# V products of a segment-recurrent attention in column tiles: two units side by side for the segment's tokens, four for the memory's, with a new order of stages

## The chip, the cores and the metric

The kernel runs on one core of one Trainium2 chip. The metric is the device time of one execution in microseconds (us). Engines: TensorE (PE, matmuls; PEld are its weight loads), VectorE (DVE), ScalarE (ACT), GpSimd (POOL) and SyncE (SP, which only issues DMA transfers here). PSUM is the memory that matmuls write, SBUF the on-chip memory that everything else works in.

## The reference

Two layers alternate, twice: A, B, A, B. A is attention over segments with a recurrent memory, B is a local dilated attention. Cut to what matters:

```python
def _A_ref(x, mem0, Wq, Wk, Wv, Wo, seg_len):       # S = 2048, Dm = 640, 32 heads of 192, M = 8, seg_len = 32
    mem = mem0
    for s in range(n_seg):                           # 64 segments, one after the other
        h = concat([mem, x[:, s*seg_len:(s+1)*seg_len]])   # 40 tokens
        q, k, v = h @ Wq, h @ Wk, h @ Wv             # each 40 x 6144
        p = softmax(where(mask, q k^T * scale, -1e9))
        o = (p v) @ Wo
        mem = o[:, :M]                               # the next segment needs it
        outs.append(o[:, M:])

def _B_ref(x, wqkv, wo):                             # 32 heads of 20, window of 8 tokens at distance 2
    ...

x = x + _A_ref(layernorm(x), ...)
x = x + _B_ref(layernorm(x), ...)
x = x + _A_ref(layernorm(x), ...)
x = x + _B_ref(layernorm(x), ...)
```

All weights are bfloat16. Wq, Wk, Wv and Wo of layer A are 31 MB together, more than fits on the chip beside the rest.

## The kernel before

The two A layers run as two **lanes** (index `l`) in one pass: lane 0 works on segment s of the first A layer, lane 1 on segment s - 2 (`LAG = 2`) of the second. So each weight that is loaded serves 2 x 40 = 80 token columns. There are 66 steps with attention (numbered 0 to 65) and one last step that only finishes layer B.

The weights of A are cut into 64 **halves** of 128 x 1920 bfloat16 (491,520 bytes): halves 0 to 31 hold Wk and Wq in turn (32 heads are 16 pairs, called units, of 384 columns), 32 to 47 Wv, 48 to 63 Wo. 31 halves stay in SBUF (`res`); 33 are streamed again in every step through a ring of five buffers (`wt`), as two DMA transfers each, which SP issues in the order of use. In step 0 all halves are read from the inputs, and the streamed ones are written back to `Wr` in the layout in which later steps read them. From then on the loads come from `Wr`.

A step is the list `ORDER`, which fixes the order of TensorE's instructions and of SP's transfers by hand; the instructions of VectorE, ScalarE and GpSimd are put in order by the framework's scheduler. Each engine works through its list strictly in order. The words of the list:

- `q0` to `q15`: K and Q of one unit, 30 matmuls of 80 columns each (L303 for q0, L308 for the others); ScalarE copies the result to one of five `QK` buffers (L310).
- `v0` to `v15`: V of one unit. The stationary operand is the state `ST`, 128 columns wide: two lanes in slots of 64, of which 40 are tokens. Five matmuls of 384 columns (L356); ScalarE copies the even units, VectorE the odd ones (L360, L362).
- `s0` to `s3`: scores of four units, in 64 x 64 and 128 x 64 tiles of the array (L320, L326), then the softmax on VectorE (L330 to L338) with the exp on ScalarE (L334).
- `t0` to `t3`: four transposes of the probabilities (L345); two copies to `PT` (L347 on VectorE, L348 on ScalarE).
- `pv0` to `pv3`: probabilities times V (L373), 128 x 64 tiles in pairs; ScalarE copies the result to `ot` (L376).
- `o0` to `o14`: the product with Wo, accumulated in `acc` (L390); o14 takes halves 62 and 63.
- Layer B: `ln1` (L278, L279), `qkv` (L438, copies L440, products L445 on VectorE and GpSimd), `logits` (L454 in 128 x 32 tiles, four side by side, softmax L465 to L473 with the exp L467 on ScalarE), `e0` to `e4` (the weights spread to all channels, L480, then product and sum on VectorE, L483 and L485), `wo` (L492), `ln2` (state of lane 1 for the next step), `store`.
- `alpha` writes the segment's tokens of lane 0 to the next `ST` on GpSimd; `input` prepares 128 tokens in every fourth step from `x_sb`, which SP loads.

At the end of a step VectorE casts the memory columns of `acc` into the next `ST` (L401); the next q0 waits for it. All PSUM tiles but `acc` come from one pool of six buffers (`ps`), used in turn. The code of the order:

```python
ORDER = """
q0 v0 q1 ln10 alpha0 q2 v1 input0 q3 v2 s0 q4 qkv0 v3 t0 q5 q6 v4 q7 v5 logits0
s1 pv0 q8 o0 o1 v6 q9 e0 t1 v7 q10 o2 o3 e1 q11 v8
s2 pv1 q12 e2 o4 o5 v9 q13 e3 t2 v10 o6 o7 q14 e4 v11 q15 v12
s3 pv2 wo0 o8 v13 v14 ln20 t3 v15 store0 o9 o10 pv3 o11 o12 o13 o14
"""
```

The functions that the change touches:

Of the kernel before, what the change touches and what calls it, by code (L numbers as in the profile page):

```python
# [10 lines left out]
BF16 = mybir.dt.bfloat16  # L11
F32 = mybir.dt.float32
# [21 lines left out]
NQK = 5  # L34
OUT_CHUNKS = ((0, 1, 2), (3, 4))
# [13 lines left out]
N_RESIDENT = 31  # L49
# [11 lines left out]
def stages():  # L61

    names = ("alpha", "ln1", "qkv", "logits", "input", "wo", "ln2", "store", "pv", "q", "s", "t", "v", "o", "e")
# [26 lines left out]
def window1(ap, c):  # L90

    v = ap[:, c, :, 0:SEG]
    dims = [list(x) for x in v.ap]
    return bass.AP(v.tensor, v.offset, dims[:2] + [[BDIL, BW]] + dims[2:])

# [11 lines left out]
class Kernel:  # L107
    def __init__(self, ctx, tc, A_x, A_mem0, A_Wq, A_Wk, A_Wv, A_Wo, B_wqkv, B_wo, out):
        self.tc, self.nc = tc, tc.nc
        self.x = A_x[0, :, :]  # L110
        self.out = out[0, :, :]
        self.S = A_x.shape[1]
        self.n_seg = self.S // SEG
        self.Wq, self.Wk, self.Wv = (w.rearrange("d h e -> d (h e)") for w in (A_Wq, A_Wk, A_Wv))
        self.Wo = A_Wo.rearrange("h e d -> (h e) d")
        self.B_wqkv, self.B_wo, self.mem0 = B_wqkv, B_wo, A_mem0[0, :, :]
        pool = lambda name, bufs, **k: ctx.enter_context(tc.tile_pool(name=name, bufs=bufs, **k))
        self.cp = pool("consts", 1)
# [6 lines left out]
        self.vp = pool("vp", 6)  # L125
        self.psC = pool("psC", 1, space=PSUM)
        self.ps = pool("ps", 6, space=PSUM)


    def constants(self):  # L130
# [47 lines left out]
        self.ST = [cp.tile([P, NCH, 2, SLOT], BF16, name=f"ST{i}") for i in range(2)]  # L178
# [5 lines left out]
        self.Pm = [cp.tile([P, 4, 2, SLOT], BF16, name=f"Pm{i}") for i in range(2)]  # L184
# [3 lines left out]
        for t in self.PT:  # L188
            nc.gpsimd.memset(t[:], 0.0)
        self.zero = cp.tile([P, NCH, SEG], BF16, name="zero")  # L190
# [8 lines left out]
        nc.vector.tensor_copy(out=self.ST[0][:, :, 0, 0:NM], in_=mt[:, :, :])  # L199
# [63 lines left out]
    def alpha_x(self, s):  # L263

        xt = self.xt[s // 4]
        o = SEG * (s % 4)
        self.nc.gpsimd.tensor_copy(out=self.ST[s % 2][:, :, 0, NM:LT], in_=xt[0][:, :, o:o + SEG])
# [27 lines left out]
    def qk(self, i):  # L295
        nc = self.nc
        st = self.ST[self.step % 2]
        ps = self.ps.tile([P, 6, 2, LT], F32, name="qk_ps", tag="ps")
        w = [self.half(2 * i + k)[:, :].rearrange("p (c n) -> p c n", c=NCH) for k in range(2)]
        if i == 0:  # L300
            for c in range(NCH):
                for m in range(6):
                    nc.tensor.matmul(ps[:, m, :, :], lhsT=w[m // 3][:, c, (m % 3) * P:(m % 3 + 1) * P], rhs=st[:, c, :, 0:LT],  # L303
                                     start=(c == 0 and m == 0), stop=(c == NCH - 1), skip_group_check=True)
        else:
            for m in range(6):
                for c in range(NCH):
                    nc.tensor.matmul(ps[:, m, :, :], lhsT=w[m // 3][:, c, (m % 3) * P:(m % 3 + 1) * P], rhs=st[:, c, :, 0:LT],  # L308
                                     start=(c == 0), stop=(c == NCH - 1))
        nc.scalar.copy(out=self.QK[i % NQK][:, 0:12 * LT], in_=ps[:, :, :, :].rearrange("p m l t -> p (m l t)"))  # L310

    def scores(self, g):
# [25 lines left out]
        nc.vector.tensor_tensor(out=self.Pm[g % 2][:, :, :, 0:LT].rearrange("p a l t -> p (a l) t"), in0=sb[:, :, :],  # L338
                                in1=sm[:, :].unsqueeze(2).to_broadcast([P, 8, LT]), op=ALU.mult)

    def p_transpose(self, g):
        nc = self.nc
        ps = self.ps.tile([P, 4, 2, SLOT], BF16, name="pt_ps", tag="ps")
        for j in range(4):
            nc.tensor.transpose(out=ps[:, j, :, :].rearrange("p h q -> p (h q)"),  # L345
                                in_=self.Pm[g % 2][:, j, :, :].rearrange("p l t -> p (l t)"), identity=self.ident[:, :])
# [3 lines left out]
    def v(self, i):  # L350
        nc = self.nc
        w = self.half(32 + i)[:, :].rearrange("p (c n) -> p c n", c=NCH)
        st = self.ST[self.step % 2]
        ps = self.ps.tile([P, UW], F32, name="v_ps", tag="ps")
        for c in range(NCH):
            nc.tensor.matmul(ps[:, :], lhsT=st[:, c, :, :].rearrange("p l t -> p (l t)"), rhs=w[:, c, :],  # L356
                             start=(c == 0), stop=(c == NCH - 1))
        vt = self.vp.tile([P, UW], BF16, name="vt")
        if i % 2 == 0:
            nc.scalar.copy(out=vt[:, :], in_=ps[:, :])  # L360
        else:
            nc.vector.tensor_copy(out=vt[:, :], in_=ps[:, :])  # L362
        self.vts[i] = vt

    def pv(self, g):
        nc = self.nc
        for k in (2 * g, 2 * g + 1):
            ps = self.ps.tile([P, 2, 3, 2, LT], F32, name="o_ps", tag="ps")
            for jj in range(2):
                i = 2 * k + jj  # L370
                vt = self.vts.pop(i)
                for (n, slot, h, col) in ((0, 0, 0, 0), (0, 1, 0, 64), (1, 0, 0, 128), (1, 1, 1, 192), (2, 0, 1, 256), (2, 1, 1, 320)):
                    nc.tensor.matmul(ps[64 * slot:64 * (slot + 1), jj, n, :, :], lhsT=vt[:, col:col + 64], rhs=self.PT[g % 2][:, i % 4, h, :, :],  # L373
# [19 lines left out]
    def finish_step(self):  # L393
        nc, s = self.nc, self.step
        nxt = self.ST[(s + 1) % 2]
# [28 lines left out]
    def b_qkv(self):  # L424
        nc = self.nc
        qT = self.w1.tile([P, NCH, 2, SEG], BF16, name="qT", tag="q")
        kh = self.w2.tile([P, NCH, 2, BPAD + SEG], BF16, name="kh")
        vh = self.w2.tile([P, NCH, 2, BPAD + SEG], BF16, name="vh")
        for new, old in ((kh, self.kh), (vh, self.vh)):
            if old is None:  # L430
                nc.gpsimd.memset(new[:, :, :, 0:BPAD], 0.0)
            else:
                nc.gpsimd.tensor_copy(out=new[:, :, :, 0:BPAD], in_=old[:, :, :, SEG:SEG + BPAD])
# [7 lines left out]
        self.qT, self.kh, self.vh = qT, kh, vh  # L441
# [63 lines left out]
    def beta_x(self):  # L505
# [4 lines left out]
        self.ln_apply(self.x2_next[:, :, :], m, r, self.ST[(self.step + 1) % 2][:, :, 1, NM:LT], SEG)  # L510
# [14 lines left out]
    def run(self):  # L525
        nc, tc = self.nc, self.tc
        self.resident, self.xt, self.vts, self.ots = {}, {}, {}, {}
        self.Wr = {h: self.dram.tile([P, HALF], BF16, name=f"Wr{h}") for h in range(N_HALVES) if h not in RESIDENT}
        self.kh = self.vh = None
        self.x2 = self.x2_next = None  # L530
        self.step = 0
        with tc.manual_schedule(engines={PE, SP}):
# [5 lines left out]
            attend = {"q": self.qk, "s": self.scores, "t": self.p_transpose, "v": self.v, "pv": self.pv, "o": self.o}  # L538
# [80 lines left out]
```

## Time and profile before

| | |
|---|---|
| median of 3 runs (lowest, highest) | 3518.95 us (3516.27, 3520.65) |
| the profiled execution: its time, its span | 3520.67 us, 3519.0 us |
| step 0 (until the first q0 of step 1 starts) | 145.4 us |
| matmuls of V, L356 | 3630 with streamed, 1650 with resident weights, 328 ns each |
| ScalarE's copies: QK (L310), ot (L376), V (L360) | 557, 559, 481 ns each |
| VectorE's copy of V (L362) | 550 ns each |
| HBM read | 1091.68 MB, 316 GB/s over the span |

The span runs from the first instruction to the last. A row of a timeline or of the chain gives the start in us, the busy time in us, the engine (PE) and source line, what is written and read, and "x" the count; in brackets stands how long the engine had been idle and what ended that. The duration of a matmul includes its way through the array: matmuls overlap, and the distance from one group's start to the next one's is what a group costs. "37 ns a pair" and the like are such distances divided by counts.

### The profile page before, as it was taken

Reading aid. Unit: us, or ns where it says so; the run is one execution under the profiler, and the core shown is the slowest. Engines: PE = TensorE matmul, PEld = TensorE weight load, DVE = VectorE, ACT = ScalarE, POOL = GpSimd, SP = SyncE. Lnnn points to the kernel's source line nnn. Section 1 sums busy time; section 2 is a strip of 40 time slices with the busy share of each in tenths; the row PEclk is TensorE's granted clock in tenths of the full one; section 3 lists DMA queues with packets and bytes.
Section 4 is the critical chain, followed back from the end, with each engine's and each line's share of the span. In section 5 each row is a group of like instructions: output and inputs, shape, how many; then the busy total and the mean of one; then the engine's idle time right before and its main releaser. Section 6 shows DMA issues by size and latency. Waiting matters only on the chain.

```text
span 3519.0 us, 172521 instructions
## 1 busy us (share of the span) xinstructions
PE 3388.8 (96%) x78044; PEld 2891.7 (82%) x78045; DVE 2197.2 (62%) x5056; ACT 1479.6 (42%) x3213; POOL 369.9 (11%) x467
## 2 busy tenths in 40 slices
PE   5799999999999999999999999999999999999997
PEld 3588888888888888888888888888888888888886
DVE  1366666666666666666666666666666666666665
ACT  1244444444444444444444444444444444444443
POOL 2110110010111011001101101110010111011000
PEclk7799999999999999999999999999999999999998
DMA  9999999999999999999999999999999999999995
GB/s 350 352 321 320 318 320 315 316 320 323 319 323 317 317 314 322 320 322 319 322 326 322 324 322 320 318 324 326 321 319 323 315 320 324 320 317 319 319 320 202
DMA packets 664961, 1121.84 MB, mean 319 GB/s; under 512 B 70744, under 2 KB 661472, under 8 KB 664224
## 3 DMA queue, kind: packets, MB, share of 16 engines
q1 hardware_dynamic: 659280, 1091.96, 92.5%
q0 software_dynamic: 2640, 16.22, 1.1%
q8 instruction: 610, 9.99, 1.1%
q10 hardware_dynamic: 2304, 2.62, 0.2%
q14 instruction: 127, 1.04, 0.1%
HBM read 1091.68 MB, written 18.84 MB: 316 GB/s over the span
## 4 chain that ended last, share of the span: by engine, by line
PE 83%; DMA 9%; DVE 4%; ACT 2%; SPq 1%; issue 1%; ACTq 0%; POOLq 0%; POOL 0%; DVEq 0%
PE qk_ps L308 29%; PE v_ps L356 21%; PE acc L390 13%; DMA wt<-Wr 4%; PE qkv_ps L438 4%; PE o_ps L373 3%; PE s_ps L326 3%; PE s_ps L320 3%; PE qk_ps L303 2%; PE bc_ps L480 2%; DMA x_sb<-in_A_x_dram 2%; PE pt_ps L345 1%; DMA wt<-in_A_Wv_dram 1%; SPq L214 1%; PE y_ps L492 1%
## 5 line engine op out<-in xcount | busy, mean ns | idle before, releaser
L310 ACT CAST QK<-qk_ps 128x480 bf16<-128x480 f32 x1056 | 581.5, 557 | 1042.7 <-PE qk_ps L308 828.5
L356 PE MATMUL v_ps<-wt,ST 128*128 128x384 bf16 x3630 | 717.4, 328 | 13.9 <-DMA wt<-in_A_Wv_dram 9.2
L308 PE MATMUL qk_ps<-ST,wt 128*128 128x80 bf16 x14850 | 687.8, 203 | 22.6 <-DMA wt<-in_A_Wq_dram 10.6
L308 PE MATMUL qk_ps<-ST,res 128*128 128x80 bf16 x14850 | 691.4, 202 | 18.1 <-DMA res<-in_A_Wq_dram 9.4
L308 PEld LDWEIGHTS <-wt 128*128 128x128 bf16 x14850 | 610.1, 100 | 78.8 <-DMA wt<-in_A_Wq_dram 11.8
L356 PEld LDWEIGHTS <-ST 128*128 128x128 bf16 x5280 | 466.1, 99 | 246.6 <-issue 16.4
L308 PEld LDWEIGHTS <-res 128*128 128x128 bf16 x14850 | 610.9, 100 | 48.9 <-DMA res<-in_A_Wq_dram 10.4
L390 PE MATMUL acc<-ot,res 128*128 128x80 bf16 x9900 | 465.6, 202 | 17.4 <-DMA res<-in_A_Wo_dram 9.6
L390 PEld LDWEIGHTS <-res 128*128 128x128 bf16 x9900 | 409.9, 100 | 38.3 <-DMA res<-in_A_Wo_dram 11.8
L362 DVE CAST vt<-v_ps 128x384 bf16<-128x384 f32 x528 | 290.2, 550 | 210.0 <-PE v_ps L356 209.8
L483 DVE TENSOR_TENSOR prod<-bc_ps,vh 128x512 bf16<-128x512 f32 x330 | 227.3, 689 | 245.0 <-PE bc_ps L480 244.4
L360 ACT CAST vt<-v_ps 128x384 bf16<-128x384 f32 x528 | 253.7, 481 | 244.8 <-PE v_ps L356 243.2
L485 DVE TENSOR_REDUCE oT<-prod 128x64 bf16<-128x512 bf16 x330 | 336.7, 1021 | 4.5
L356 PE MATMUL v_ps<-res,ST 128*128 128x384 bf16 x1650 | 326.8, 329 | 2.7 <-DMA res<-in_A_Wv_dram 2.7
L390 PE MATMUL acc<-ot,wt 128*128 128x80 bf16 x5940 | 309.9, 202 | 6.2 <-DMA wt<-in_A_Wo_dram 3.5
L376 ACT CAST ot<-o_ps 128x480 bf16<-128x480 f32 x528 | 268.4, 559 | 109.3 <-PE o_ps L373 109.3
L330 DVE TENSOR_TENSOR sb<-s_ps,maskA 128x320 f32<-128x320 f32 x264 | 129.7, 491 | 253.7 <-PE s_ps L326 253.6
L390 PEld LDWEIGHTS <-wt 128*128 128x128 bf16 x5940 | 261.3, 100 | 18.1 <-issue 4.7
L445 POOL TENSOR_TENSOR prod<-qT,kh 128x1280 bf16<-128x1280 bf16 x66 | 169.9, 2575 | 653.0 <-ACT kh L440 653.0
L348 ACT COPY PT<-pt_ps 64x320 bf16<-64x320 bf16 x264 | 110.9, 420 | 296.7 <-DVE PT L347 295.1
L273 POOL TENSOR_TENSOR sq<-x 128x160 f32<-128x160 bf16 x64 | 28.9, 452 | 1837.4 <-DVE x L496 1837.4
L445 DVE TENSOR_TENSOR prod<-qT,kh 128x1280 bf16<-128x1280 bf16 x66 | 201.2, 3048 | 3.4 <-ACT kh L440 3.4
(117 smaller groups left out, 3709.3 us busy)
## 6 DMA issues: line engine op xcount, KB each, us to landing
wt<-Wr SPq DMA_DIRECT2D x4290, 240.0 KB, 4.8
Wr<-wt POOLq DMA_DIRECT2D x33, 480.0 KB, 6.7
wt<-in_A_Wv_dram SPq DMA_DIRECT2D x11, 480.0 KB, 10.5
res<-in_A_Wo_dram SPq DMA_DIRECT2D x10, 480.0 KB, 10.8
wt<-in_A_Wk_dram SPq DMA_DIRECT2D x9, 480.0 KB, 11.1
res<-in_A_Wq_dram SPq DMA_DIRECT2D x9, 480.0 KB, 11.3
res<-in_A_Wk_dram SPq DMA_DIRECT2D x7, 480.0 KB, 10.2
wt<-in_A_Wq_dram SPq DMA_DIRECT2D x7, 480.0 KB, 10.2
```

The source lines that it names most:

```text
L308: nc.tensor.matmul(ps[:, m, :, :], lhsT=w[m // 3][:, c, (m % 3) * P:(m % 3 + 1) * P], rhs=st[:, c, :, 0:LT], start=(c == 0), stop=(c == NC ...
L310: nc.scalar.copy(out=self.QK[i % NQK][:, 0:12 * LT], in_=ps[:, :, :, :].rearrange("p m l t -> p (m l t)"))
L330: nc.vector.tensor_tensor(out=sb[:, :, :], in0=sv, in1=self.maskA[:, :].unsqueeze(1).to_broadcast([P, 8, LT]), op=ALU.add)
L356: nc.tensor.matmul(ps[:, :], lhsT=st[:, c, :, :].rearrange("p l t -> p (l t)"), rhs=w[:, c, :], start=(c == 0), stop=(c == NCH - 1))
L360: nc.scalar.copy(out=vt[:, :], in_=ps[:, :])
L362: nc.vector.tensor_copy(out=vt[:, :], in_=ps[:, :])
L376: nc.scalar.copy(out=ot[:, :, :, :], in_=ps[:, :, :, :, :].rearrange("p j n l t -> p (j n) l t"))
L390: nc.tensor.matmul(a[:, at, :, :], lhsT=w[h][:, m, dc * P:(dc + 1) * P], rhs=self.ots[h // 2][:, 3 * (h % 2) + m, :, :], start=(h == 0 and ...
L438: nc.tensor.matmul(ps[:, d, :, :], lhsT=self.wqkv[:, c, kind * D + d * P:kind * D + (d + 1) * P], rhs=self.xnB[:, c, :].rearrange("p (l t) ...
L445: eng.tensor_tensor(out=self.prod[:, :, l, :, :], in0=qT[:, :, l, :].unsqueeze(2).to_broadcast([P, NCH, BW, SEG]), in1=window(kh, l), op=A ...
L483: nc.vector.tensor_tensor(out=pv, in0=ps[:, :, :, :], in1=window1(self.vh, c), op=ALU.mult)
L485: nc.vector.tensor_reduce(out=self.oT[:, c, :].rearrange("p (l t) -> p l t", l=2), in_=pv.rearrange("p l w t -> p l t w"), op=ALU.add, axi ...
```

## The change

Three things change together, and two follow from them.

1. **Token layout.** `ST` becomes 96 columns wide: 16 columns of zeros, then 40 tokens with the two lanes interleaved (token 0 of lane 0, token 0 of lane 1, and so on): columns 16 to 31 are the memory of both lanes, 32 to 95 the segments of both. q reads 80 contiguous columns, and its ScalarE copy puts the lanes apart again while it reads PSUM.
2. **V in column tiles.** For each group g of four units there are three stages. `va` and `vb` take two units each: the 64 segment columns are the stationary operand of two tiles, 128 x 64 at array columns 0 and 64, and each tile is fed its own unit's weights. `vc` takes the 32 columns of zeros and memory with four units in 128 x 32 tiles. Results go to one buffer `V` with rows chosen per unit (`SEG_ROW`, `MEM_ROW`); all eight copies of a group are on ScalarE. The probabilities are written to the matching columns of `Pm` in two VectorE operations instead of one, and `PT` is made by two VectorE operations that mask by lane, in place of one copy each on VectorE and ScalarE.
3. **New order and 32 resident halves.** V stands in one block behind each s and pv, so the other stages move; 32 halves stay in SBUF, 32 are streamed, another set than before: of Wv only 33, 35, 38, 41 and 46. `kh` and `vh` of layer B become fixed buffers instead of two that alternate, and GpSimd copies their tails in place.

```diff
-N_RESIDENT = 31
+N_RESIDENT = 32
+PAD = 2 * NM
+MID = 2 * PAD
+WIDE = PAD + 2 * LT
+SEG_ROW = (0, 64, 0, 64)
+MEM_ROW = (64, 0, 96, 32)
...
 ORDER = """
-q0 v0 q1 ln10 alpha0 q2 v1 input0 q3 v2 s0 q4 qkv0 v3 t0 q5 q6 v4 q7 v5 logits0
-s1 pv0 q8 o0 o1 v6 q9 e0 t1 v7 q10 o2 o3 e1 q11 v8
-s2 pv1 q12 e2 o4 o5 v9 q13 e3 t2 v10 o6 o7 q14 e4 v11 q15 v12
-s3 pv2 wo0 o8 v13 v14 ln20 t3 v15 store0 o9 o10 pv3 o11 o12 o13 o14
+q0 q1 ln10 alpha0 q2 input0 q3 s0 va0 vb0 vc0 qkv0 q4 t0 q5 q6 q7
+s1 pv0 va1 vb1 vc1 logits0 q8 o0 q9 t1 o1 e0 q10 o2 e1 o3 q11
+s2 pv1 va2 vb2 vc2 e2 q12 o4 q13 e3 t2 q14 o5 e4 q15 wo0
+s3 pv2 va3 vb3 vc3 o6 o7 ln20 store0 t3 o8 o9 pv3 o10 o11 o12 o13 o14
 """
...
-STREAMED = (
-    0, 2, 5, 7, 8, 9, 11, 12, 14, 16, 18, 21, 22, 25, 27, 30, 34, 35, 37, 38, 39, 40, 42, 43, 44, 45, 47, 53, 54,
-    56, 58, 60, 63,
-)
+STREAMED = (1, 5, 6, 7, 8, 11, 13, 14, 15, 17, 22, 23, 25, 26, 29, 30, 31, 33, 35, 38, 41, 46, 48, 49, 50, 51, 53, 55, 56, 58, 60, 63)
...
+def tokens(t):
+
+    return t[:, :, PAD:].rearrange("p c (t l) -> p c l t", l=2)
...
-        nc.scalar.copy(out=self.QK[i % NQK][:, 0:12 * LT], in_=ps[:, :, :, :].rearrange("p m l t -> p (m l t)"))
+        nc.scalar.copy(out=self.QK[i % NQK][:, 0:12 * LT].rearrange("p (m l t) -> p m l t", m=6, l=2), in_=ps[:, :, :, :].rearrange("p m t l -> p m l t"))
...
-        nc.vector.tensor_tensor(out=self.Pm[g % 2][:, :, :, 0:LT].rearrange("p a l t -> p (a l) t"), in0=sb[:, :, :],
-                                in1=sm[:, :].unsqueeze(2).to_broadcast([P, 8, LT]), op=ALU.mult)
+        at = [P * j + SEG_ROW[j] for j in range(4)]
+        am = [P * j + MEM_ROW[j] + PAD for j in range(4)]
+        for o, t, n in ((at, NM, SEG), (am, 0, NM)):
...
+            nc.vector.tensor_tensor(out=out, in0=strip(sb[:, :, :], t, [[4 * LT, 2], [2 * LT, 2], [1, n], [LT, 2]]),
+                                    in1=strip(sm[:, :], 0, [[4, 2], [2, 2], [0, n], [1, 2]]), op=ALU.mult)
...
-        nc.vector.tensor_copy(out=self.PT[g % 2][0:64, :, :, 0, :], in_=ps[0:64, :, :, 0:LT])
-        nc.scalar.copy(out=self.PT[g % 2][64:128, :, :, 1, :], in_=ps[64:128, :, :, 0:LT])
+        for l in range(2):
+            nc.vector.tensor_scalar(out=self.PT[g % 2][:, :, :, l, :], in0=ps[:, :, :, 0:LT], scalar1=self.maskL[:, l:l + 1], scalar2=None, op0=ALU.mult)
...
-        for c in range(NCH):
-            nc.tensor.matmul(ps[:, :], lhsT=st[:, c, :, :].rearrange("p l t -> p (l t)"), rhs=w[:, c, :],
-                             start=(c == 0), stop=(c == NCH - 1))
...
+    def v_seg(self, g, a):
...
+        for c in range(NCH):
+            for j in units:
+                r = SEG_ROW[j]
+                nc.tensor.matmul(ps[r:r + 64, :], lhsT=st[:, c, MID:WIDE], rhs=self.wv[j][:, c, :],
+                                 start=(c == 0), stop=(c == NCH - 1), tile_position=(0, r), skip_group_check=True)
+        for j in units:
+            r = SEG_ROW[j]
+            nc.scalar.copy(out=self.V[r:r + 64, j, :], in_=ps[r:r + 64, :])
+
+    def v_mem(self, g):
...
+        for c in range(NCH):
+            for j in range(4):
+                r = MEM_ROW[j]
+                nc.tensor.matmul(ps[r:r + 32, :], lhsT=st[:, c, 0:MID], rhs=self.wv[j][:, c, :],
+                                 start=(c == 0), stop=(c == NCH - 1), tile_position=(0, r), skip_group_check=True)
+        for j in range(4):
+            r = MEM_ROW[j]
+            nc.scalar.copy(out=self.V[r:r + 32, j, :], in_=ps[r:r + 32, :])
```

The words of the new list stand for `va`, `vb` (`v_seg` with a = 0 and 1) and `vc` (`v_mem`) of one group; the others mean what they meant before.

More of the change, by code (lines that the diff above doesn't have):

```diff
@@ L183, in constants @@
             nc.gpsimd.memset(t[:, 12 * LT:], 0.0)
-        self.Pm = [cp.tile([P, 4, 2, SLOT], BF16, name=f"Pm{i}") for i in range(2)]
+        self.Pm = [cp.tile([P, 4, P], BF16, name=f"Pm{i}") for i in range(2)]
         for t in self.Pm:
@@ L297, in qk @@
         st = self.ST[self.step % 2]
-        ps = self.ps.tile([P, 6, 2, LT], F32, name="qk_ps", tag="ps")
+        ps = self.ps.tile([P, 6, LT, 2], F32, name="qk_ps", tag="ps")
         w = [self.half(2 * i + k)[:, :].rearrange("p (c n) -> p c n", c=NCH) for k in range(2)]
@@ L426, in b_qkv @@
         qT = self.w1.tile([P, NCH, 2, SEG], BF16, name="qT", tag="q")
[L427 to L433, printed above, removed]
+        kh, vh = self.kh, self.vh
+        if self.step > 1:
+            for t in (kh, vh):
+                nc.gpsimd.tensor_copy(out=t[:, :, :, 0:BPAD], in_=t[:, :, :, SEG:SEG + BPAD])
         for kind, dst in enumerate((qT[:, :, :, :], kh[:, :, :, BPAD:], vh[:, :, :, BPAD:])):
```

56 lines of the change are left out of this document (32 added, 24 removed).

## The prediction

> **What bounds the kernel now.** I read the page's chain of work first, then the transfer queue, one middle step in the windows view, the same step in the chain in order of time, and the timelines of single engines around the places that the change touches.
>
> ```profile
> PE 3388.8 (96%) x78044; PEld 2891.7 (82%) x78045; DVE 2197.2 (62%) x5056; ACT 1479.6 (42%) x3213; POOL 369.9 (11%) x467
> PE 83%; DMA 9%; DVE 4%; ACT 2%; SPq 1%; issue 1%; ACTq 0%; POOLq 0%; POOL 0%; DVEq 0%
> q1 hardware_dynamic: 659280, 1091.96, 92.5%
> ```
>
> TensorE carries the chain, with the weight stream close behind. One middle step (span, busy times, clock, DMA share, GB/s):
>
> ```profile
> 1489.47:1540.40 50.93, 50.47 (x1184) 43.28 (x1182) 32.72 (x77) 22.02 (x48) 5.14 (x6) 1.00 0.96 322
> ```
>
> 322 GB/s at a share of 0.96 gives an estimate of 335 GB/s for a full stream: 33 halves of 491,520 bytes need 48.4 us of a step, 32 need 46.9. Step 0 ends at 145.4 us, the 65 attending steps end at 3489.4, so a step takes 51.45 us; 30 us of tail follow.
>
> ```profile
> 1494.88 1.07 PE qk_ps L308 x30
> 1495.96 0.81 PE v_ps L356 x5
> 1496.77 0.36 PE s_ps L320 x16
> ...
> 1505.93 0.81 PE v_ps L356 x5
> 1506.74 0.39 PE lg_ps L454 x20
> ...
> 1507.86 0.44 PE o_ps L373 x24
> 1508.30 1.18 PE qk_ps L308 x30
> ```
>
> This is the price list: q 1.07 us (36 ns a matmul), one V unit 0.81 (163 ns for 384 columns), and hardly a hole. Now the followers:
>
> ```profile
> 1512.36 0.70 PE L308 MATMUL qk_ps<-ST,res 128*128 128x80 bf16 x15
> 1512.90 0.38 PE L480 MATMUL bc_ps<-attn,ET 128*128 128x512 bf16 x1
> 1513.10 0.56 ACT L310 CAST QK<-qk_ps 128x480 bf16<-128x480 f32 x1 [0.60 <-PE qk_ps L308]
> ```
>
> After q9 has issued (1512.90) its copy starts 0.20 us later and takes 0.56: a q's result is readable 0.76 us after its last matmul. Today a V unit (0.81) stands in nearly every such gap.
>
> **The gain.** V now takes 5 matmul passes per unit, 20 for four; afterwards 5 pairs, 5 pairs and 5 quadruples: 15 passes. Do tiles run side by side? L373 is pairs of 64-column tiles, some with different moving operands: 24 matmuls of 80 columns in 0.44 us, 37 ns a pair, against 36 for one full matmul. L454 is quadruples of 32-column tiles with four different operands: 20 in 0.39 us with its exit, 5 x 56 ns without. So a pair or quadruple costs a pass: 4 x 5 x 0.163 = **-3.26 us** a step.
>
> Changes of tile shape cost about 0.095 us (q after pv 1.18 against 1.07; s after V starts 0.91 after V's start, not 0.81, at 1495.79 and 1496.70 of the timeline). New: one between vb and vc in each group, plus vc's exit, minus those that s and pv no longer need because V follows them in their own shape, and in group 1 logits follows vc in its shape: 3 more a step, **+0.29**. Net **-2.97**.
>
> **What loses its cover.** (a) s0, s1, s2 now stand directly behind q3, q7, q11. Their fourth unit needs that q's copy: ready at 0.76 + 0.06 (least gap from another engine's end to PE's start in these rows, Pm to pt_ps at L345) = 0.82; PE reaches that unit at 0.095 + 0.20 = 0.30. Behind it in PE's queue waits everything. 0.52 each, **+1.56**. (L320's sixteen take 0.25 without their exit; three units of four, 0.20.) s3 is covered by wo0. The copy now reads PSUM with a stride. No ScalarE row shows that; DVE's strided PSUM reduce (L465, 281 ns) costs no more than a plain operation of its size (L466, 292), its strided SBUF reduce 1.46 times (L275 709, L336 486). I take no extra; the other end is 0.26 x 3 = 0.8 a step.
>
> (b) e0. All eight V copies go to ScalarE, ahead of the exp of logits in its order.
>
> ```profile
> 1505.99 0.50 ACT L360 CAST vt<-v_ps 128x384 bf16<-128x384 f32 x1
> 1506.37 0.59 ACT L310 CAST QK<-qk_ps 128x480 bf16<-128x480 f32 x1
> ```
>
> The next operation starts 0.37 to 0.38 after a V copy. From s1's end: exp of s at 1.77 (0.20, then 0.53, 0.52, 0.49 of DVE), copies from 2.14 to 5.10, exp of logits to 5.41, then L469, L470 and four L473 (0.40 + 0.27 + 1.14) to 7.25, PE at 7.30. PE itself: pv0 0.43, va and vb 1.64, vc 0.91, logits 0.39, q8 1.07, o0 0.54, q9 1.07, t1 0.22, o1 0.54 = 6.83. **+0.47**. Without the eight copies it would be ready at 6.5.
>
> (c) wo0 moves from four stages behind e4 to one q behind it.
>
> ```profile
> 1475.32 0.38 PE L480 MATMUL bc_ps<-attn,ET 128*128 128x512 bf16 x1
> ...
> 1475.74 0.69 DVE L483 TENSOR_TENSOR prod<-bc_ps,vh 128x512 bf16<-128x512 f32 x1 [1.56 <-PE bc_ps L480]
> 1476.46 1.02 DVE L485 TENSOR_REDUCE oT<-prod 128x64 bf16<-128x512 bf16 x1
> ```
>
> (first line PE, the others DVE). 2.16 us from e4's matmul to oT, plus 0.06; PE offers 0.22 + 1.07 and four chunks of wo0 (0.12). **+0.82**; DVE, with two PT operations before it, is free just then, so up to 1.1.
>
> (d) t3 to pv3 shrinks from 1.9 us to 1.07, and both PT halves are serial DVE work behind ln2's: 0.1, at most 0.4. **+0.1**. (e) x_sb is issued on SP behind half 63, whose ring slot is now freed by vc3, about 0.6 us later against the step's end. Every fourth step DVE holds the state copy behind it ("PE qk_ps L303 <- DVE ST L401: 14.4" in 14 waits): 0.6 more in one of four, **+0.17**.
>
> Hidden: ScalarE's load rises from 22 us to some 29 of 51 (less 8 x 0.38 for old V copies and 4 x 0.42 for PT, plus 32 x 0.37); ssq is ready 2.24 us after q0 starts and PE now asks at 2.30; POOL's vh copy waits for e4, but behind it stands only sq of x2, later still; Pm in two strided pieces has over 1 us of slack; PSUM buffers come round in time in all four stages; the added set-up lies in step 0, which the stream bounds. Step 0 writes back one half less, -1.5 us once.
>
> The Trainium skill, page "TensorEngine Tiling (Array Packing)", section "PSUM Bottleneck", speaks against this edit: tiling speeds TensorE and not the evacuation, which may become the limit, and both engines should evacuate. Its section "Restrictions" adds that column tiling disables the fast weight load; the trace shows no exposed load, since L454 takes in four weight sets every 56 ns. By the first rule the sum would be that of the ScalarE rival below, 3650; by the rows ScalarE binds nowhere but in (b).
>
> (f) The stream. About 1 us of a step is lost now, 0.26 of it to x_sb, the rest mostly late halves. 32 halves ask 46.9 of some 51 us, a little easier; but q7, q11 and q15 now need two streamed halves within 0.54 us, while one takes 1.47 us to stream, and SP now issues 33 and 35 together, to be held until vc0. From minus 0.5 to plus 0.6; I take **+0.25**.
>
> Sum: -2.97 + 1.56 + 0.47 + 0.82 + 0.1 + 0.17 + 0.25 = **+0.40 us** a step, x 65 = 26, less 1.5: span 3519.0 + 24.5. The profiled execution took 3520.67, 1.7 above its span and also above the median of 3518.95; on the median: **3544 us**. Bounds of (a) to (f), not all at once, give 3500 to 3590.
>
> **Rivals.** *The stream's waits go (faster).* PE now pauses five times a step and the ring refills: if the late halves vanish, about 0.7 a step, and the +0.25 does not come, the sum is -0.55 a step: 3519 - 37 = 3482. It decides once the halves of q7, q11 and q15 land before need. For: 4 us of slack a step against 3. Against: the paired needs. *e0 and wo0 keep their cover*, if DVE and ScalarE run ahead of my ledger: 1.29 a step less waiting and no stream loss give -1.14: 3443. Against: (c) is nearly pure latency. *ScalarE becomes the bound of V*: 8 x 0.37 = 2.96 us of copies against 2.55 of matmuls, 0.41 in each group if six PSUM buffers do not carry it: 1.6 a step, 3650. Against: ScalarE has caught up by the second q after each V by my ledger. *The tiles do not overlap for 384 columns*: 40 passes, 20 x 4 x 0.163 = 13 us a step, 4370; L373 and L454 speak against it.
>
> **Chances.** Forecast 0.52 (a tenth of the whole within 0.2%, about what can be told from no change), stream 0.20, cover 0.14, ScalarE 0.09, no overlap 0.02, rest slower 0.03. Faster 0.34, same 0.10, slower 0.56. The range takes the rivals in but for the last: 3440 to 3650; the forecast's own is 3500 to 3590.
>
> **What would show it.** In the changed profile: five passes of va, vb, vc each in about 0.82 us; PE idle at the s line with ScalarE's QK copy as releaser, 0.5 us, three a step; PE's e0 waiting for attn, wo0 for oT. If those waits are missing I am wrong towards faster; if "wt<-Wr" leads PE's waits, (f) was too small; if v_ps waits for V copies, ScalarE is the bound.

## The result, and the profile after

The changed kernel takes **3632.4 us** (median of 4 runs, 3625.0 to 3648.1), the kernel before 3517.6 (4 runs): ratio **1.0335, 95% interval 1.0293 to 1.0378**. The forecast was 3544 us: the direction is right, the loss is 115 us instead of 26, and the time lies above the forecast's own range of 3500 to 3590. The profiled execution took 3648.06 us, span 3646.3, 127 us more than the profiled execution before; its steps (the mean of steps 3 to 64) take 53.36 us instead of 51.42, and 65 x 1.94 = 126.

The page of after: busy times, the chain by engine, the weight queue.

```profile
PE 3293.8 (90%) x83325; PEld 2826.4 (78%) x83325; DVE 1994.9 (55%) x5057; ACT 2084.7 (57%) x4533; POOL 378.9 (10%) x467
PE 56%; DMA 16%; DVE 11%; ACT 10%; issue 4%; SPq 3%; POOL 0%; ACTq 0%; POOLq 0%; DVEq 0%
q1 hardware_dynamic: 640560, 1060.00, 88.4%
```

TensorE has 95 us less to do and carries 56% of the chain instead of 83%. What it lost went to three followers. The windows view of one middle step says the same (columns as before: span, busy times, clock, DMA share, GB/s):

```profile
1751.83:1804.65 52.82, 48.91 (x1263) 42.12 (x1260) 29.62 (x76) 31.29 (x68) 5.27 (x6) 1.00 0.93 305
```

The weight queue streams less (305 GB/s against 322), so it has more room on average; yet transfers stand in the chain with 16% instead of 9. The waits view names the places (total us, times, longest us):

```profile
PE bc_ps L515 <- DVE attn L508: 77.1, 66, 3.0
PE s_ps L340 <- ACT QK L330: 76.1, 196, 0.7
PE qk_ps L328 <- DMA wt<-Wr: 45.1, 107, 2.2
PE y_ps L527 <- DVE oT L520: 17.4, 34, 1.9
```

The third of these rows in the kernel before:

```profile
PE qk_ps L308 <- DMA wt<-Wr: 6.9, 22, 0.5
```

e0 waits for attn in every step, the scores for the QK copy three times a step, and the wait of q for streamed halves ("wt<-Wr") has grown from 6.9 us to 45.1. The first two in TensorE's timeline:

```profile
1768.94 0.24 PE L340 MATMUL s_ps<-QK 64*64 64x40 bf16 x4 [0.41 <-ACT QK L330]
...
1777.62 0.39 PE L515 MATMUL bc_ps<-attn,ET 128*128 128x512 bf16 x1 [1.25 <-DVE attn L508]
```

and the queue of ScalarE in front of e0's exponential:

```profile
1771.16 0.47 ACT L354 ACTIVATE sb<-sb 128x320 f32<-128x320 f32 x1 [0.33 <-DVE sb L353]
1771.54 1.95 ACT L389 CAST V<-v_ps 64x384 bf16<-64x384 f32 x4
1773.39 1.95 ACT L402 CAST V<-v_ps 32x384 bf16<-32x384 f32 x4
1775.36 0.31 ACT L502 ACTIVATE sbb<-sbb 128x128 f32<-128x128 f32 x1
```

The eight copies take 3.82 us from the first to the exponential, 0.48 each. The prediction had 0.37.

V itself does what it promised. Two units of a pair run side by side:

```profile
1758.87 0.33 PE L385 MATMUL v_ps<-res,ST 128*64 128x384 bf16 x1
1758.87 0.33 PE L385 MATMUL v_ps<-wt,ST 128*64 128x384 bf16 x1
```

Both units start at 1758.87, and the next pair at 1759.03: 0.163 us a pair on average. From start to start the V groups take 10.66 us a step instead of 13.52: -2.86.

### The profile page after: what moved, and what is told of

Its sections match the earlier page's. It is cut to its first block, busy times and chain, and to the rows that moved or that the text cites. A ratio compares the mean times of both kernels' runs of the same rounds, so it can differ in the third digit from the quotient of the medians.

```text
span 3646.3 us, 185054 instructions
## 1 busy us (share of the span) xinstructions
PE 3293.8 (90%) x83325; PEld 2826.4 (78%) x83325; DVE 1994.9 (55%) x5057; ACT 2084.7 (57%) x4533; POOL 378.9 (10%) x467
## 4 chain that ended last, share of the span: by engine, by line
PE 56%; DMA 16%; DVE 11%; ACT 10%; issue 4%; SPq 3%; POOL 0%; ACTq 0%; POOLq 0%; DVEq 0%
PE qk_ps L328 18%; DMA wt<-Wr 12%; PE v_ps L385 9%; PE acc L428 8%; PE v_ps L398 5%; ACT V L389 3%; PE qkv_ps L473 3%; ACT V L402 3%; ACT QK L330 3%; PE s_ps L346 2%; PE o_ps L411 2%; DVE oT L520 2%; PE qk_ps L323 2%; PE s_ps L340 2%; SPq L250 2%
## 5 line engine op out<-in xcount | busy, mean ns | idle before, releaser
L328 PE MATMUL qk_ps<-ST,wt 128*128 128x80 bf16 x15840 | 718.8, 203 | 62.6 <-DMA wt<-Wr 45.1
L328 PEld LDWEIGHTS <-wt 128*128 128x128 bf16 x15840 | 628.4, 100 | 96.8 <-DMA wt<-Wr 64.9
L328 PEld LDWEIGHTS <-res 128*128 128x128 bf16 x13860 | 562.4, 101 | 39.8 <-issue 10.4
L389 ACT CAST V<-v_ps 64x384 bf16<-64x384 f32 x1056 | 495.8, 469 | 150.5 <-PE v_ps L385 131.4
L428 PE MATMUL acc<-ot,wt 128*128 128x80 bf16 x9900 | 498.4, 202 | 17.6 <-DMA wt<-in_A_Wo_dram 8.5
L402 ACT CAST V<-v_ps 32x384 bf16<-32x384 f32 x1056 | 494.7, 468 | 22.5 <-PE v_ps L398 3.2
L385 PE MATMUL v_ps<-res,ST 128*64 128x384 bf16 x3630 | 488.6, 331 | 13.0 <-DMA res<-in_A_Wv_dram 12.1
L428 PEld LDWEIGHTS <-wt 128*128 128x128 bf16 x9900 | 420.6, 100 | 33.0 <-issue 11.1
L385 PEld LDWEIGHTS <-ST 128*64 128x64 bf16 x5280 | 286.5, 112 | 132.8 <-issue 26.5
L385 PE MATMUL v_ps<-wt,ST 128*64 128x384 bf16 x1650 | 320.1, 330 | 7.5 <-DMA wt<-in_A_Wv_dram 6.1
L480 POOL TENSOR_TENSOR prod<-qT,kh 128x1280 bf16<-128x1280 bf16 x66 | 204.8, 3103 | 742.9 <-ACT kh L475 742.9
L428 PEld LDWEIGHTS <-res 128*128 128x128 bf16 x5940 | 251.4, 100 | 32.1 <-issue 28.1
L398 PE MATMUL v_ps<-res,ST 128*32 128x384 bf16 x3630 | 266.3, 331 | 0.0
L398 PE MATMUL v_ps<-wt,ST 128*32 128x384 bf16 x1650 | 264.5, 331 | 0.4 <-issue 0.4
```

The source lines that it names most:

```text
L385: nc.tensor.matmul(ps[r:r + 64, :], lhsT=st[:, c, MID:WIDE], rhs=self.wv[j][:, c, :], start=(c == 0), stop=(c == NCH - 1), tile_position=( ...
L389: nc.scalar.copy(out=self.V[r:r + 64, j, :], in_=ps[r:r + 64, :])
L398: nc.tensor.matmul(ps[r:r + 32, :], lhsT=st[:, c, 0:MID], rhs=self.wv[j][:, c, :], start=(c == 0), stop=(c == NCH - 1), tile_position=(0, ...
L402: nc.scalar.copy(out=self.V[r:r + 32, j, :], in_=ps[r:r + 32, :])
L428: nc.tensor.matmul(a[:, at, :, :], lhsT=w[h][:, m, dc * P:(dc + 1) * P], rhs=self.ots[h // 2][:, 3 * (h % 2) + m, :, :], start=(h == 0 and ...
L480: eng.tensor_tensor(out=self.prod[:, :, l, :, :], in0=qT[:, :, l, :].unsqueeze(2).to_broadcast([P, NCH, BW, SEG]), in1=window(kh, l), op=A ...
```

## The experiments

All changes are against the changed kernel, except in the last run. "Late halves" is the time between the matmuls inside one q, o or V group that goes beyond their usual pitch; "s waits" and "e0" are the same inside s and in front of e0. All such columns are us a step, means of steps 3 to 64 from the starts of TensorE's matmuls in the profiled execution. Ratios are to the kernel before, timed beside each run.

| run | median us | ratio (95%) | step | s waits | e0 | late halves | clock |
|---|---|---|---|---|---|---|---|
| before | 3517.6 | 1 | 51.42 | 0 | 0 | 0.70 | 0.985 |
| after | 3632.4 | 1.0335 (1.0293 to 1.0378) | 53.36 | 1.54 | 1.31 | 1.98 | 0.982 |
| split copies | 3814.6 | 1.0851 (1.0818 to 1.0883) | 56.31 | 1.55 | 1.48 | 1.65 | 0.973 |
| no pairs | 3577.8 | 1.0165 (1.0148 to 1.0182) | 52.19 | 1.54 | 1.37 | 0.40 | 0.984 |
| less Wo | 3608.4 | 1.0251 (1.0236 to 1.0266) | 52.78 | 1.54 | 1.29 | 1.23 | 0.983 |
| va before s | 3647.0 | 1.0357 (1.0328 to 1.0387) | 53.54 | 0.0 | 0.64 | 2.78 | 0.982 |
| V tiles | 3637.5 | 1.0336 (1.0303 to 1.0368) | 53.16 | 1.56 | 1.32 | 1.87 | 0.983 |
| V tiles, split | 3813.9 | 1.0839 (1.0803 to 1.0875) | 55.82 | 1.53 | 1.52 | 1.44 | 0.977 |
| s one q later | 3687.8 | 1.0479 (1.0429 to 1.0528) | 54.03 | 0.04 | 2.21 | 2.42 | 0.970 |
| logits before V | 3671.4 | 1.0433 (1.0401 to 1.0465) | 53.71 | 1.53 | 0.0 | 3.15 | 0.977 |
| order alone | 3590.9 | 1.0202 (1.0183 to 1.0221) | 52.65 | 0.0 | 0.0 | 3.22 | 0.983 |
| order and stream | 3493.2 | 0.9935 (0.9915 to 0.9955) | 51.20 | 0.02 | 0.0 | 1.01 | 0.977 |
| input load later | 3461.2 | 0.9836 (0.9815 to 0.9858) | 50.57 | 0.04 | 0.0 | 1.11 | 0.981 |
| before, ring of six | 3543.7 | 1.0079 (1.006 to 1.0097) | 51.96 | 0 | 0 | 0.54 | 0.979 |

### The paired halves

My theory of the stream: q7, q11 and q15 need two streamed halves within 0.54 us, and the second is late. So does q3 (halves 6 and 7), which the prediction did not name. All four second halves are left to a resident one, so part of Q is computed with other weights:

```diff
+INSTEAD = {7: 4, 15: 12, 23: 20, 31: 28}
+        if h in INSTEAD and self.step > 0:
+            return self.resident[INSTEAD[h]]
```

> The changed kernel, but from step 1 on halves 7, 15, 23 and 31 (Q weights, second halves of q3, q7, q11, q15) are not loaded: resident halves 4, 12, 20 and 28 are used in their place, so that part of the Q products is computed with other weights; 28 halves are streamed. Theory (lateness belongs to q stages that need two streamed halves): the waits in the second half of q3, q7, q11 and q15 fall from 1.09 us a step to below 0.2; wo0's wait for oT, which q15's wait now hides, grows from 0.29 to about 0.8; net -0.5 to -0.7 us a step, -33 to -45 us: near 3593 us. Rival (the stream is late wherever it is, by its load): the same gain as in the run without four Wo halves.

Its control takes the same number of bytes off the stream in Wo, away from the pairs (`INSTEAD = {49: 52, 51: 54, 56: 57, 60: 59}`):

> The control: the changed kernel, but from step 1 on halves 49, 51, 56 and 60 (Wo for o1, o3, o8, o12) are not loaded and resident 52, 54, 57 and 59 are used in their place, so that part of the last product has other weights; 28 halves are streamed, the pairs stay. Theory of the pairs: the waits in the second halves of q7, q11 and q15 keep at least 0.6 of their 0.99 us a step; time down by no more than 25 us, 3607 or above. Rival (load): they go as in the other run, 3590 to 3600 us.

With no pairs the waits of q on streamed halves are gone; 45.1 us in total become (waits view of TensorE; L327 is q0's line in this run, and the line of the other q has no such row)

```profile
PE qk_ps L327 <- DMA wt<-Wr: 0.4, 1, 0.4
```

and the median falls by 55 us, more than the 33 to 45 expected; with the same bytes taken from Wo it falls by 24, and the second halves of q7, q11 and q15 keep 0.80 of their 0.99 us. So 31 us hang on the pairs, and the load as such is worth the rest. By steps: late halves lose 1.58 us, and wo0, which the late half of q15 had covered, waits 0.83 instead of 0.29: 65 x (1.58 - 0.54) = 68 us of the 81 by which the two profiled executions differ.

### Who holds up e0: the eight copies

```diff
-            nc.scalar.copy(out=self.V[r:r + 64, j, :], in_=ps[r:r + 64, :])
+            (nc.scalar.copy if j % 2 == 0 else nc.vector.tensor_copy)(out=self.V[r:r + 64, j, :], in_=ps[r:r + 64, :])
```

(the same for the four copies of 32 rows)

> The changed kernel with one edit: the V copies of odd units go to VectorE, those of even units stay on ScalarE. Theory (e0 waits because eight V copies at 0.49 us stand ahead of the exp of logits on ScalarE): four copies leave that queue, VectorE gets four of 0.47 to 0.55 us in front of its part of the same chain; PE's wait before e0 falls from 1.31 to 0.4 to 0.7 us a step, the other waits stay; about -0.75 us a step, -49 us: near 3583 us. Rival (VectorE's own chain sets e0): the wait stays above 1.1 and the time within 15 us of 3632.

It lost 182 us to the changed kernel, and e0 waited longer instead of shorter. In ScalarE's waits the copies of the two engines stood one behind the other, and I took the one tile V for the reason. So V became four tiles, with ScalarE alone and with the copies split as above:

```diff
-        self.V = cp.tile([P, 4, UW], BF16, name="V")
+        self.V = [cp.tile([P, UW], BF16, name=f"V{j}") for j in range(4)]
```

> Same computation, same order as the changed kernel; only the one tile V[P, 4, UW] becomes four tiles of [P, UW], one for each unit, all eight copies of a group still on ScalarE. Theory A (the copies follow each other at 0.49 instead of 0.37 us because they write one tile and are chained by it): the eight copies take 8 x 0.37 = 3.0 instead of 3.9 us, the wait ahead of e0 falls from 1.31 to about 0.35 us a step, and the time from 3632 to about 3632 - 65 x 0.95 = 3570 us. Rival B (the pitch of 0.49 comes from the change of partitions between neighbouring copies, whatever tile they write): pitch, e0's wait and the time stay where they are, 3620 to 3645 us.

> Four V tiles, one for each unit, as in the run beside it, and the copies of the odd units on VectorE: the split of the copies without the one tile that chained both engines. Theory (the loss of the first split came from the shared tile): four copies stand ahead of the logits' exponential on ScalarE instead of eight, it starts about 1.9 us earlier, and e0's wait of 1.31 us a step goes to 0 to 0.2; s waits 1.54 as before; time 3632 - 65 x 1.1 = about 3560 us (3540 to 3590). Rival (the loss came from VectorE's queue, in which the copies stand ahead of the softmax): the steps stay near 56 us, 3780 to 3820 us.

Both theories fell, and both times the rival's range was met: 3637 us with ScalarE alone, 3814 with the split. The waits view of ScalarE in the second run, with four V tiles:

```profile
ACT V L403 <- DVE V L403: 417.1, 264, 2.2
```

That is the 416.1 us which the run with one V tile had in the same place. What the two engines still share in that run is the PSUM tile v_ps that all four copies read; no run gave each engine a PSUM tile of its own. But this is idle time of ScalarE. TensorE waits elsewhere, in front of pv3 and wo0 (its waits in the first split run):

```profile
PE o_ps L411 <- ACT ln_r L256: 94.2, 64, 1.6
PE y_ps L527 <- DVE oT L520: 73.0, 67, 1.9
```

pv3 reads PT, and VectorE's timeline of the second split run shows what stands ahead of it after s3:

```profile
1818.96 0.49 DVE L357 TENSOR_REDUCE sm<-sb 128x8 f32<-128x320 f32 x1 [0.54 <-ACT sb L355]
1819.48 0.56 DVE L390 CAST V<-v_ps 64x384 bf16<-64x384 f32 x1
1820.07 0.20 DVE L358 RECIPROCAL sm<-sm 128x8 f32<-128x8 f32 x1
1820.31 0.56 DVE L390 CAST V<-v_ps 64x384 bf16<-64x384 f32 x1
1820.88 0.56 DVE L364 TENSOR_TENSOR Pm<-sb,sm 128x256 bf16<-128x256 f32 x2
1821.47 0.55 DVE L403 CAST V<-v_ps 32x384 bf16<-32x384 f32 x1
...
1822.55 0.55 DVE L403 CAST V<-v_ps 32x384 bf16<-32x384 f32 x1 [0.44 <-ACT V L403]
...
1823.70 0.67 DVE L374 TENSOR_SCALAR PT<-pt_ps,maskL 128x320 bf16<-128x320 bf16 x2
```

PT ends at 1824.37 and pv3 starts at 1824.42 (the releaser named above, ln_r of ScalarE, ends at 1824.40). From the start of sm to the end of PT it takes 5.44 us on average instead of 3.40, and VectorE is idle for 0.66 of them instead of 0.85: the difference is its four copies. So the rival of the second run is what the trace shows, the copies stand in VectorE's queue ahead of the softmax and of PT. Against the run with four tiles and ScalarE alone pv3 waits 1.3 us a step longer, wo0 0.9 and t3 0.5; the steps differ by 2.66.

The pitch of 0.48 us is not the V tile's. Starts of neighbouring copies when ScalarE was never idle between them, medians in ns:

| from, to | rows | PSUM tile | one V tile | four V tiles |
|---|---|---|---|---|
| unit 1 to unit 2 | 64 to 0 | changes | 498 | 500 |
| unit 2 to unit 3 | 0 to 64 | same | 496 | 498 |
| unit 3 to the first memory copy | 64 to 64 | changes | 378 | 379 |
| memory copy to memory copy | each another | same | 490 to 495 | 492 to 497 |

Only where the start row stays is a copy 0.12 us cheaper, whatever tile is read or written. Before, every V copy and its neighbours started at row 0, and 0.37 came from there. From the first copy to the exponential the start row changes seven times of eight, 7 x 0.12 = 0.84 us: the whole of e0's error (1.31 less 0.47).

The Trainium skill, "TensorEngine Tiling (Array Packing)", section "PSUM Bottleneck", wants both engines to evacuate. The traces do not bear that out for this kernel: the split cost 182 us, since VectorE's copies stood ahead of what TensorE waited for.

### Moving the waits away one by one

The scores wait for the QK copy. First the segment pair va was put in front of s0, s1 and s2:

```diff
-q0 q1 ln10 alpha0 q2 input0 q3 s0 va0 vb0 vc0 qkv0 q4 t0 q5 q6 q7
-s1 pv0 va1 vb1 vc1 logits0 ...
+q0 q1 ln10 alpha0 q2 input0 q3 va0 s0 vb0 vc0 qkv0 q4 t0 q5 q6 q7
+va1 s1 pv0 vb1 vc1 logits0 ...
```

> The changed kernel with va0, va1 and va2 moved in front of s0, s1 and s2 (and pv), nothing else. Theory (s waits for the ScalarE copy of the q right before it): 0.82 us of matmuls cover the copy, PE's waits in s fall from 1.54 us a step to below 0.1, and each move adds one or two changes of tile shape, 0.1 to 0.2 us each time: -1.0 to -1.25 us a step, less up to 0.3 that the stream takes back: -45 to -80 us, 3550 to 3587 us. Rival (ScalarE is the bound): the wait moves to pv or q copies and the time stays within 20 us of 3632.

(In this order va1, va2 write V before pv0, pv1 read it, so parts of two groups' products are taken with the next group's values.) The s waits are gone, 1.54 to 0, and e0 waits 0.64 instead of 1.31; pv now waits 0.67 for the V copies, which must come first in this order, and late halves grow from 1.98 to 2.78. The time, 3647 us, can't be told from that of the changed kernel: the two intervals overlap. Then two orders without that fault. In one, q4, q8 and q12 stand ahead of s0, s1 and s2:

> Only the order: q4, q8 and q12 are issued ahead of s0, s1 and s2 instead of behind (t0 ahead of q5), so that each score group has a whole q of 1.07 us between the last QK that it reads and itself. Everything else as in the changed kernel. Theory: the s waits go from 1.54 to 0.1 us a step or less (3632 - 94 = 3538 us), and the weight stream takes part of it back, as it did when a V pair was put there (0.8 us a step): the halves at q4, q8, q12 and vb0 are needed about 1.1 us earlier than they were. 3545 to 3600 us. Rival (the stream sets the step and takes all of it back): 3620 to 3650 us, with the waits between q matmuls above 2 us a step.

It was 56 us slower than the changed kernel. I had overlooked that q8 had stood between logits0 and e0: e0's wait rose from 1.31 to 2.21. And something came on top that no sum of waits holds. TensorE's timeline, and the windows view of the same stretch (the last three columns: granted clock, DMA share, GB/s):

```profile
1908.82 0.70 PE L428 MATMUL acc<-ot,wt 128*128 128x80 bf16 x15
1911.85 0.39 PE L515 MATMUL bc_ps<-attn,ET 128*128 128x512 bf16 x1 [2.32 <-DVE attn L508]
1912.07 2.05 PE L328 MATMUL qk_ps<-ST,res 128*128 128x80 bf16 x30
```

```profile
1911.00:1912.00 1.00, 0.15 (x1) 0.11 (x2) 0.94 (x4) 0.00 (x0) 0.00 (x0) 1.00 1.02 386
1912.00:1913.00 1.00, 1.00 (x18) 0.93 (x17) 1.00 (x3) 0.00 (x0) 0.00 (x0) 0.62 0.97 351
...
1914.00:1915.00 1.00, 1.00 (x18) 1.00 (x16) 0.14 (x1) 0.56 (x1) 0.00 (x0) 0.50 0.13 32
...
1916.00:1917.00 1.00, 1.00 (x34) 1.00 (x31) 0.96 (x2) 0.00 (x0) 0.00 (x0) 1.00 0.79 192
```

After 2.3 us without work the clock is granted at half for 3.4 us: 18 matmuls in a microsecond instead of 34. The record of the granted clock has 33 such windows of 3413 ns in this run between 200 us and the end of the last step with attention, 31 of them right behind e0; 5 in the changed kernel, one of them behind three waits of about half a us each; none before. Not every long wait is followed by one: e0 waited over 1.9 us in 45 steps of that stretch, and 30 of these waits were. An estimate of the windows' price: 33 x 3.41 / 2 = 56 us, 48 more than in the changed kernel. The Trainium skill, "TensorE: Matmul & The Clock Gate", section "Part 1: The HAM clock gate (the "warmup" mystery)", has windows of 3413 ns and half the clock after an idle one; the traces agree on the length and the half. They differ in what is enough: here about 2 us of idle time often sufficed, not a whole idle window.

The other order moves logits0 from behind vc1 to ahead of va1, past the copies in ScalarE's queue:

> Only the order: logits0 moves from behind vc1 to just ahead of va1, so that the exponential of the logits stands ahead of the eight V copies in ScalarE's queue instead of behind them. Theory (e0's wait is the ScalarE queue of V copies): e0's wait goes from 1.31 to 0.0 to 0.2 us a step, s and the stream stay, time 3632 - 65 x 1.2 = about 3555 us (3540 to 3585). Rival (the copies, now later, hold the PSUM buffers and move the wait to q9 or t1): the e0 wait goes and the same time shows up as waits of q, t or o on the v_ps or qk_ps copies, 3600 to 3640 us.

e0's wait went to nothing, as expected, and the time rose by 39 us. The waits that the rival expected (for the copies out of PSUM) did not come; the stream took it:

```profile
PE qk_ps L328 <- DMA wt<-Wr: 97.8, 184, 3.0
```

The second half of q11, behind e0, now waits 1.00 us a step instead of 0.18. While TensorE stood at e0, the ring filled; without that rest the pair (22, 23) is late, and behind the longer waits there are 14 stretches at half clock (16 windows).

### All of them at once, without and with a new stream

The order with all the moves (q4, q8, q12 ahead of the scores, logits0 behind pv0, o6 between e4 and q15), first alone:

> The order of the run beside it alone: the ring of five and the streamed halves stay as in the changed kernel. Theory (what an order wins in waits for ScalarE is given back to the weight stream unless the streamed halves are chosen for that order): s, e0 and wo0 lose about 3.1 us a step, late halves grow from 2.0 to 3.5 us or more, and waits of over 2 us on a half bring clock windows at half speed; 3500 to 3600 us. Rival (the stream has room): late halves stay near 2.0 and the time falls to 3632 - 65 x 3.1 = about 3430 us.

```profile
PE qk_ps L328 <- DMA wt<-Wr: 86.7, 159, 2.0
```

The time lies in the range given: the 2.85 us of s and e0 are gone (wo0 still waits 0.29), and late halves went from 1.98 to 3.22 (3.5 or more had been expected). That alone would be 1.61 us a step less; it is 0.71, and of the rest 0.47 stands in pv. Then with the stream made for it:

```diff
-RING = 5
+RING = 6
-STREAMED = (1, 5, 6, 7, 8, 11, 13, 14, 15, 17, 22, 23, 25, 26, 29, 30, 31, 33, 35, 38, 41, 46, 48, 49, 50, 51, 53, 55, 56, 58, 60, 63)
+STREAMED = (1, 2, 5, 7, 8, 9, 10, 11, 13, 15, 16, 17, 19, 20, 23, 24, 25, 27, 30, 31, 34, 43, 47, 48, 50, 52, 53, 54, 56, 57, 58, 61)
-        sb = self.w2.tile([P, 8, LT], F32, name="sb")
+        sb = self.w1.tile([P, 8, LT], F32, name="sb")
```

(mx and sm likewise; one Pm and one PT instead of two)

> Every wait that was found, at once. Order: q4, q8, q12 ahead of s0, s1, s2; logits0 behind pv0; o6 between e4 and q15. Stream: a ring of six halves instead of five (paid for by single tiles for the scores, the probabilities and their transposes, which are read before they are written again), and 32 streamed halves chosen anew for this order, so that nearly each lands over 2 us before it is needed by a count of 1.467 us a half. Theory (the step of 53.4 us is 47.6 us of work and the waits named): s, e0 and wo0 lose about 3.1 us a step, late halves fall from 2.0 to under 1.0, granted clock 0.98 or more since no wait is longer than 1 us: a step of 48.5 to 50.0 us, 3320 to 3420 us. Rival A (the clock falls because the denser V passes leave TensorE less rest, not because of long waits): the waits go too, but the granted clock stays at 0.97 or falls, 3400 to 3480 us. Rival B (32 halves of 1.467 us in 49 us can't be fed): late halves of 3 us a step or more, 3480 us or more.

3493 us, faster than the kernel before, and 98 us below the order alone: the streamed set and the ring together are what let the order pay; no run took them apart. It missed its range by 73 us, and the clock fell to 0.977 as Rival A had it. Waits and chain show why, in the view of DVE's waits and its timeline of one fourth step, and in PE's:

```profile
DVE bst L269 <- DMA x_sb<-in_A_x_dram: 40.5, 16, 10.5
```

```profile
754.21 0.20 DVE L357 RECIPROCAL sm<-sm 128x8 f32<-128x8 f32 x1
756.42 0.49 DVE L269 BATCH_NORM_STATS2 bst<-x_sb 128x6 f32<-128x320 bf16 x1 [2.01 <-DMA x_sb<-in_A_x_dram]
756.83 0.54 DVE L363 TENSOR_TENSOR Pm<-sb,sm 128x256 bf16<-128x256 f32 x2
```

```profile
PE pt_ps L370 <- DVE Pm L363: 25.5, 14, 3.0
```

In every fourth step the statistics of the next x tile stand in VectorE's queue between sm and Pm of s3, and wait there for a transfer. t3 waits, pv3 waits, and 11 of this run's 12 stretches at half clock follow at that place. So the clock falls behind long waits here, and not for the denser passes of Rival A. One line moves the load past the ring's next halves:

```diff
-                if s % 4 == 1 and 4 * (s // 4 + 1) < self.n_seg:
-                    self.input_load(s // 4 + 1)
                 for what, i in PLAN:
+                    if (what, i) == ('q', 2) and s % 4 == 1 and 4 * (s // 4 + 1) < self.n_seg:
+                        self.input_load(s // 4 + 1)
```

> The run with the new order and the ring of six, with one line moved: the load of the next x tile is issued in front of q2 of its step instead of at the step's start, so that VectorE's bn_stats on that tile stand behind the ln2 work in its queue, in the stretch in which it is idle, and no longer between sm and Pm of s3. Theory (in every fourth step VectorE waits about 2 us for that load, t3 and pv3 wait for VectorE, and the long wait costs a clock window at half speed on top): the 14 waits of t3 go (25.5 us), those of pv3 behind them (13.3 us), and the clock rises from 0.977 to 0.984 (about 20 us): 3493 - 55 = about 3440 us (3420 to 3465). Rival (the clock falls because of the denser passes, and the load's wait only moves to the step's boundary): the clock stays at 0.977 and the time within 15 us of 3493.

```profile
DVE bst L269 <- DMA x_sb<-in_A_x_dram: 13.8, 15, 2.4
PE qk_ps L328 <- DMA wt<-Wr: 5.2, 15, 0.8
PE 69%; DVE 12%; DMA 7%; ACT 6%; issue 4%; SPq 2%; POOL 1%; ACTq 0%; POOLq 0%; DVEq 0%
```

(Waits of DVE and of PE, and the chain by engine.) **3461 us, 1.6% faster than the kernel before**: 32 of the 55 us expected, inside the range; t3's waits are gone, the stretches at half clock fall from 12 to 3. By an estimate from the same starts about 2.5 us of waits a step remain.

Is that the V products or the ring? The kernel before with a ring of six and nothing else (paid for in the same way):

> A control: the kernel before, in its own order with its own V products and its own 33 streamed halves, and only the ring made six halves deep (paid for in the same way, and by a row of zeros that is broadcast). Theory (before waits only about 0.7 us a step for halves, and a deeper ring can win no more than that): 3518 - 65 x 0.3 to 0.7 = 3470 to 3500 us, so that the new V products with their waits taken away stay ahead of it by 30 us or more. Rival (what won in the new version was the ring, not the V products): 3450 us or less.

It became slower, which neither side expected. Its waits of DVE and PE:

```profile
DVE bst L249 <- DMA x_sb<-in_A_x_dram: 44.5, 16, 11.5
PE o_ps L373 <- ACT PT L348: 36.0, 14, 3.7
```

Late halves do fall, 0.70 to 0.54 us a step. But in this run, too, the x tile's statistics moved, from behind ln2's work to a place ahead of PT (VectorE's timeline):

```profile
761.66 0.49 DVE L249 BATCH_NORM_STATS2 bst<-x_sb 128x6 f32<-128x320 bf16 x1 [3.36 <-DMA x_sb<-in_A_x_dram]
...
762.99 0.31 DVE L347 COPY PT<-pt_ps 64x320 bf16<-64x320 bf16 x1
```

pv3 waits for it in every fourth step, with 11 half-clock windows. So the ring with the single tiles that pay for it wins nothing by itself, but this is no fair ceiling of the old V: the kernel before with that load moved as well was not run. The steps of the kernel before hold some 1.2 us of waits in all, 50.2 us of work; the best version has 48.0 of work and 2.5 of waits. By that estimate the old V without a single wait, 50.2 us a step, would be level with the new one as it stands, 50.57. That is not tried on the chip, so how much of the 1.6% is owed to the V products stays open.

## Why the prediction was right and wrong

By its own steps, us a step:

| step | predicted | measured | |
|---|---|---|---|
| V in three passes, shape changes | -2.97 | -2.75 | the V groups alone -2.86; pairs and quadruples cost a pass, a shape change 0.095 as taken |
| (a) s behind its QK copy | 1.56 | 1.54 | three waits of about half a us; no extra for the strided read |
| (b) e0 | 0.47 | 1.31 | mis-sized: 0.48 a copy, not 0.37 |
| (c) wo0 | 0.82 | 0.29 | the late half of q15, 0.59, stands in front of it |
| (d) t3 to pv3 | 0.1 | 0.22 | |
| (e) x_sb at the boundary | 0.17 | -0.13 | |
| (f) stream | 0.25 | 1.28 | mis-sized: the pairs |
| sum | 0.40 | 1.94 | 0.18 of it in small waits; "issue" grew from 19 to 37 us in all |

The direction is right, since (a) with the rest eats the gain as it said. The size is not: 3632 us is outside the forecast's own range, and only the wide range holds it, which reached to 3650 for the ScalarE rival. That rival did not happen, so this part is luck. Two terms carry the miss. In (b) the price of a copy was read from a row in which every copy starts at row 0; the new copies start elsewhere. The trace of before had a sign of it: behind L348's copy, which starts at row 64 and takes 0.42 us, the next operation came 0.45 us after its start, behind a V copy of 0.48 us it came after 0.37. In (f) the paired halves were named, and then priced by the average load of the stream, with 0.6 as the upper end; it became 1.28, and the run without pairs takes 1.58 us a step off the late halves. In (c) the sum was good and the place taken: with no pairs wo0 waits 0.83, close to the 0.82 predicted.

The rivals: the stream's waits did not go; e0 and wo0 did not keep cover; ScalarE is not the bound of V, since v_ps waits nowhere for a copy (no such line among PE's waits), though 3650 was near by chance; the tiles do overlap. The stream rival had the ring refill in TensorE's pauses. What the prediction did not have is the other side of that, that the waits stand in for each other: of three orders that took one wait away two were slower and one was no faster, with more late halves in each. Nor did it have the clock, by which a rest of about 2 us can be charged again.

## What to carry to other kernels

When an engine that waits in several places feeds on a stream near its limit, price the stream's late pieces by the shortest distance between two of them, and test waits together: one taken away alone comes back at the next streamed piece. A load that is issued in program order on a busy queue has its place in every other engine's queue as well; look at who stands behind its first reader. A wait of 2 us on TensorE can cost nearly twice its length: two thirds of e0's long waits did in the run with s one q later.

## What the hardware showed that I had not expected

- ScalarE copies of 384 columns follow each other at 0.38 us if both start at the same row and at 0.48 to 0.50 if not, for 32 and 64 rows, whichever tiles they read and write.
- The granted clock can fall to one half for a window of 3.41 us after some 2 us of idle time: 33 such windows are an estimated 56 us of one run (clock 0.970 against 0.982 in the changed kernel).
- VectorE's product of q and the window keys takes 0.83 us after the change (L480) and took 3.05 before (L445), with the same shape; GpSimd's half of it went from 2.58 to 3.10. The engine that starts first decides. One step of before, then one of after:

```profile
1500.84 3.08 DVE L445 TENSOR_TENSOR prod<-qT,kh 128x1280 bf16<-128x1280 bf16 x1
1500.67 2.57 POOL L445 TENSOR_TENSOR prod<-qT,kh 128x1280 bf16<-128x1280 bf16 x1 [9.70 <-ACT kh L440]
```

```profile
1764.85 0.83 DVE L480 TENSOR_TENSOR prod<-qT,kh 128x1280 bf16<-128x1280 bf16 x1 [2.30 <-ACT kh L475]
1764.89 3.11 POOL L480 TENSOR_TENSOR prod<-qT,kh 128x1280 bf16<-128x1280 bf16 x1 [11.56 <-ACT kh L475]
```

  In all 924 pairs of the 14 profiled executions VectorE takes 0.83 us where it starts 0.04 to 0.11 us ahead of GpSimd, and about 3.06 where it starts 0.08 to 0.17 us behind. The new tiles kh and vh are not the reason: the two split runs have them and the slow form. No run changed the order of the two alone.
